# A retention and phase-mixing kernel on one core: the third pair of chunks is loaded ahead of the token weights, and the orders of the first batch are rewritten for it

## The chip, the core and the metric

The kernel runs on one core of one Trainium2 chip. Its engines work side by side, each through its own list of instructions in order: TensorE (PE in the profile, its weight loads PEld), VectorE (DVE), ScalarE (ACT), GpSimd (POOL) and SyncE (SP), which here issues the transfers. An engine waits for another through semaphores. The metric is the device time of one execution in microseconds, as the median of several runs; a profile of one execution tells what each engine did at each moment. The time before is 168.54 us (median of 3 runs, 168.21 to 168.79).

## What is computed

Two layers follow each other. The first is a retention recurrence over 768 tokens for each of 4 batches and 8 heads of 64; the second mixes its output `x` (4 x 768 x 512) over tokens, through weights that are multiplied with cosine and sine of `x @ w_theta`:

```python
for t in range(S):                                   # retention, per batch and head
    state = gamma * state + einsum('bhd,bhe->bhde', k[:, :, t], v[:, :, t])
    y[:, :, t] = scale * einsum('bhd,bhde->bhe', q[:, :, t], state)
x = y.transpose(0, 2, 1, 3).reshape(B, S, H * D)

theta = x @ w_theta                                  # phase mixing
zr, zi = x * cos(theta), x * sin(theta)
u = x + einsum('ts,bsd->btd', w_tok_r, zr) + einsum('ts,bsd->btd', w_tok_i, zi)
out = u + maximum(u @ w_ch, 0.0)
```

All inputs and the output are float32; the kernel computes in bf16 with float32 sums.

## The kernel before

The 768 tokens of a batch are 3 pairs of chunks (a chunk is 128 tokens), so there are 12 pairs, n = 0 to 11; pairs 0 to 2 are batch 0. The output has 24 tiles of 128 tokens, m = 0 to 23; the tiles of a batch need z of all its six chunks, and all token weights.

What a pair goes through, by the names of the code: `load` brings k, q and v (512 KB each). `prep` casts k to bf16 and multiplies q and v with powers of gamma (tile `kqb`); `DP` means half on DVE and half on POOL, `PP` both halves on POOL. `flip` transposes k or q on TensorE into PSUM (`kq_ps`) and copies it to `kqT`. `ret_A` makes the scores of one half of the pair, `ret_mask` masks them on DVE, `ret_Y` multiplies them with v, `ret_I` adds what comes from the state of earlier chunks, `ret_S` adds to the state and `state_out` copies it (ACT). `ret_out` copies the result to `xT`; `x_pe` transposes it back to `x_sb`; `theta` is the product with w_theta and its cosine and sine (ACT); `zmul` makes z on DVE.

What a tile goes through: `w_cast` and `w_flip` bring one row of 128 of both token weights to bf16 (POOL) and transpose it (TensorE); `moe_M(m, lo, hi)` adds the products of tile m with z of chunks lo to hi-1 (two products of 512 columns each); `moe_u` adds x; `moe_U` transposes u; `moe_O` is the product with w_ch; `moe_out` makes the output tile `ot`; `store` writes it. `keep_busy` issues products of zeros that nobody reads.

PSUM buffers are shared by tags: all transposes and the outputs of `moe_O` take turns in two buffers of the tag `tr`; retention results and theta in two of `acc`; scores have one (`at`), the state one (`st`), token products one (`y`).

```python
    def load(n, name):
        b, g = divmod(n, nG)
        t = io.tile([P, H, 2 * D], FT, name="pair", bufs=7)
        ...
    def load_wtok(r, t0):
        src = (moe_w_tok_r, moe_w_tok_i)[r]
        t = io.tile([P, S], FT, name="wtok", bufs=4)
        ...
    # p: k, q, v of a pair; w: a row of both token weights; th, ch: w_theta, w_ch
    loads("p0 th p1 w0 p2 w1 w2 p3 w3 ch p4 w4 p5 w5")
    ...
    DV, PL, AC = nc.vector, nc.gpsimd, nc.scalar
    DP, PP = (DV, PL), (PL, PL)
    ... # pair 0
    theta(0, 0)
    flip(1, "k")
    theta(0, 1)
    flip(1, "q")
    prep(1, "v", PP)
    w_cast(0)
    x_pe(0, None)
    ret_A(1, 0)
    ret_mask(1, 0)
    x_out(0, DV.tensor_copy)
    keep_busy(3)
    ret_S(1, 0)
    ... # rest of pair 1, with w_flip(0, 0) in it
    w_flip(1, 0)
    prep(2, "k", (PL,))
    zmul(0, 0)
    flip(2, "k")
    prep(2, "q", DP)
    theta(1, 0)
    zmul(0, 1)
    theta(1, 1)
    moe_M(0, 0, 1)
    flip(2, "q")
    prep(2, "v", PP)
    w_cast(1)
    w_cast(2)
    x_pe(1, AC.copy)
    moe_M(0, 1, 2)
    ret_A(2, 0)
    ret_mask(2, 0)
    ... # rest of pair 2, then token products of tiles 0 and 1, flips of pair 3

    for n in range(nG, B * nG + 1):         # n = 3 to 12
        mine, done = tiles_of[n], tiles_of[n - 1]
        ...
        if n == nG:
            nc.gpsimd.tensor_copy(wch, wdma["ch"])
        ...
        if n in pairs:
            ret_A(n, 0)
            ret_mask(n, 0)
        if n == nG:
            moe_M(0, 5, nT)
            w_flip(1, 2)
            moe_u(0)
            moe_M(1, 4, nT)
            moe_u(1)
        ...
        moe_M(first, 0, 3 if two else 2)
        ... # state, second scores, Y of pair n
        if n < U_DMA:
            moe_U(done)
        if n == nG:
            prep(n + 1, "k", (AC,))
            preps(DP)                       # q and v of pair n+1, and a w_cast
        if n == nG or n + 1 < K_DMA and not two:
            moe_M(first, 2, 4)
        if n < nG + 3:
            w_tok(n - nG + 3)               # both w_flips of a row
        if not two:
            moe_M(first, 4, nT)
            moe_u(first)
        for i, t in enumerate(done):
            if n == nG:
                flip(n + 1, "kq"[i])
            moe_O(t)
            moe_out(t)
        ...
```

Of the kernel before, what the change touches and what calls it, by code (L numbers as in the profile page):

```python
# [32 lines left out]
def kernel(  # L33
# [57 lines left out]

    def load_wtok(r, t0):
        src = (moe_w_tok_r, moe_w_tok_i)[r]
        t = io.tile([P, S], FT, name="wtok", bufs=4)
        nc.sync.dma_start(out=t, in_=src[t0 * P:(t0 + 1) * P, :])
        wdma[r, t0] = t

    def loads(order):
        for what in order.split():
            if what == "th":  # L100
                load_w512("th", moe_w_theta)
            elif what == "ch":
                load_w512("ch", moe_w_ch)
            elif what[0] == "w":
                for r in range(2):
                    load_wtok(r, int(what[1:]))
            else:
                for name in "kqv":
                    load(int(what[1:]), name)

    loads("p0 th p1 w0 p2 w1 w2 p3 w3 ch p4 w4 p5 w5")


    warm = const.tile([P, dm], BF)
# [72 lines left out]
            copy(t, ps)  # L187
        st[n, name + "T"], st[n, name + "_ps"] = t, ps

    def flip_out(n, name):  # L190
        nc.vector.tensor_copy(st[n, name + "T"], st[n, name + "_ps"])

    def flip_dma(n, name):
        t = work.tile([P, 2, NP, P], BF, name="kqT", bufs=6)
# [109 lines left out]
    def x_out(n, copy):  # L304
        b, g = divmod(n, nG)
        copy(xs[b][:, 2 * g:2 * g + 2, :],
             st[n, "x_ps"].rearrange("p a j e -> p a (j e)"))

    def theta(n, a):
        th_ps = psum.tile([P, dm], FT, name="th_ps", tag="acc", bufs=2)  # L310
        for j in range(NP):
            nc.tensor.matmul(th_ps, st[n, "xT"][:, a, j, :], wth[:, j, :], start=(j == 0),  # L312
                             stop=(j == NP - 1))
        cs = work.tile([P, 2, dm], BF, name="cs", bufs=3)
        nc.scalar.activation(cs[:, 0, :], th_ps, AF.Sin, bias=halfpi, scale=1.0)  # L315
        nc.scalar.activation(cs[:, 1, :], th_ps, AF.Sin, bias=zerob, scale=1.0)  # L316
        st[n, "cs", a] = cs
# [53 lines left out]

    def moe_out(m):
        b, t0 = divmod(m, nT)
        ot = work.tile([P, dm], FT, name="ot", bufs=8)
        nc.vector.scalar_tensor_tensor(ot, mo[m]["o"], 0.0, mo[m]["u"], ALU.max, ALU.add)  # L375
        mo[m]["ot"] = ot

# [6 lines left out]
    def w_cast(t0):  # L384
        for r in range(2):
            row = work.tile([P, S], BF, name="wrow", bufs=5)
            nc.gpsimd.tensor_copy(row, wdma[r, t0])  # L387
            wrow[r, t0] = row
# [73 lines left out]
    def keep_busy(times):  # L462
        for _ in range(times):
            nc.tensor.matmul(warm_ps, warm[:, 0:P], warm, start=True, stop=True)
# [35 lines left out]
    theta(0, 1)  # L500
    flip(1, "q")
    prep(1, "v", PP)
    w_cast(0)
    x_pe(0, None)
    ret_A(1, 0)
    ret_mask(1, 0)
    x_out(0, DV.tensor_copy)
    keep_busy(3)
    ret_S(1, 0)
    state_out(1, 0)  # L510
# [1 line left out]
    ret_mask(1, 1)  # L512
    ret_Y(1, 0)
    ret_I(1, 0)
    w_flip(0, 0)
    ret_S(1, 1)
    state_out(1, 1)
    ret_I(1, 1)
    ret_Y(1, 1)
    ret_out(1, 0, AC.copy)  # L520
    ret_out(1, 1, DV.tensor_copy)
    w_flip(1, 0)
    prep(2, "k", (PL,))
    zmul(0, 0)
    flip(2, "k")
    prep(2, "q", DP)
    theta(1, 0)
    zmul(0, 1)
    theta(1, 1)
    moe_M(0, 0, 1)  # L530
    flip(2, "q")
    prep(2, "v", PP)
    w_cast(1)
    w_cast(2)
    x_pe(1, AC.copy)
    moe_M(0, 1, 2)
    ret_A(2, 0)
    ret_mask(2, 0)
    ret_S(2, 0)
    state_out(2, 0)  # L540
    ret_A(2, 1)
    ret_mask(2, 1)
    zmul(1, 0)
    ret_Y(2, 0)
    ret_I(2, 0)
    ret_I(2, 1)
    w_flip(0, 1, False)
    w_flip(1, 1, False)
    ret_Y(2, 1)
    ret_out(2, 0, AC.copy)  # L550
    ret_out(2, 1, DV.tensor_copy)
    w_out(0, 1)
    w_out(1, 1)
    zmul(1, 1)
    prep(3, "k", (PL,))
    moe_M(0, 2, 3)
    theta(2, 0)
    flip(3, "k")
    prep(3, "q", DP)
    theta(2, 1)  # L560
    moe_M(0, 3, 4)
    x_pe(2)
    w_flip(0, 2, False)
    w_out(0, 2, AC.copy)
    moe_M(1, 0, 2)
    zmul(2, 0)
    flip(3, "q")
    prep(3, "v", PP)
    w_cast(3)
    moe_M(1, 2, 4)  # L570
    zmul(2, 1)
    moe_M(0, 4, 5)


    tiles_of = {nG - 2: [], nG - 1: [0, 1]}
# [16 lines left out]
    for n in range(nG, B * nG + 1):  # L592
# [17 lines left out]

        if n == nG:
            nc.gpsimd.tensor_copy(wch, wdma["ch"])
        if nG + 3 < n + 1 < Q_DMA:
            preps(PP)
        if late:
# [2 lines left out]
        if n in pairs:  # L618
            ret_A(n, 0)
            ret_mask(n, 0)  # L620
        if n == nG:
            moe_M(0, 5, nT)
            w_flip(1, 2)
            moe_u(0)
            moe_M(1, 4, nT)
            moe_u(1)
        if late:
            ret_Y(n - 1, 1)
            ret_S(n - 1, 1)
# [12 lines left out]
            load(n + 3, "q")  # L642

        first = mine[0]
        moe_M(first, 0, 3 if two else 2)
        if late:
            theta(n - 1, 0)
            if n - 1 < X_DMA:
# [27 lines left out]
            moe_U(done)  # L676
        if n == nG:
            prep(n + 1, "k", (AC,))
            preps(DP)
        if n == nG or n + 1 < K_DMA and not two:  # L680
            moe_M(first, 2, 4)
        early_z = late and n < nG + 3
        if early_z and n > nG + 1:
            zmul(n - 1, 0)
        if n < nG + 3:
            w_tok(n - nG + 3)
        if early_z:
            zmul(n - 1, 0 if n == nG + 1 else 1)
# [14 lines left out]
        if two and n in pairs:  # L703
            moe_u(mine[1])
        for i, t in enumerate(done):
            if n == nG:
                flip(n + 1, "kq"[i])
            moe_O(t)
            moe_out(t)
        if late and not early_z:  # L710
# [48 lines left out]
```

## Time and profile before

| What | Value |
|---|---|
| Time, median of 3 runs | 168.54 us |
| Span of the profiled execution | 166.5 us |
| TensorE busy | 155.2 us |
| VectorE busy | 102.4 us |
| ScalarE busy | 79.1 us |
| GpSimd busy | 66.6 us |
| Granted clock of TensorE | full, in all slices |
| Moved by DMA, mean | 38.45 MB, 231 GB/s |

"Busy" counts the time in which an engine had at least one instruction in work. Products on TensorE are pipelined: one of 512 columns is listed with 379 ns, while the next one starts 0.22 us later. The page cuts the span into 40 slices of 4.16 us and shows each engine's busy share in tenths. The timeline lists instructions by start and length, with the idle time ahead of them and what ended it in square brackets.

Some moments in the timeline of TensorE serve as marks. The first scores of pair 1 start at 18.34 us, those of pair 2 at 27.38, those of pair 3 at 38.25. The first iteration of the loop (n = 3) ends, and the next begins, with the `ret_I` at 48.41.

### The profile page before, as it was taken

How to read it: one execution, taken by the hardware profiler on the slowest of the kernel's cores; microseconds unless marked ns; L12 is line 12 of the kernel's file. 1: busy time of each engine (PE TensorE's matmuls, PEld its weight loads, DVE VectorE, ACT ScalarE, POOL GpSimd, SP SyncE). 2: the span in 40 equal slices, each digit the busy share in tenths (PEclk: the TensorE clock that was granted, in tenths of full speed). 3: DMA queues.
4: the chain of work that ended last, by engine and by line, in shares of the span. 5: the costliest groups of instructions: out<-in, count | busy, mean ns of one | idle time of the engine just before them, and what ended most of it. 6: DMA issues, size and time to landing. Idle time of an engine off the chain costs nothing.

```text
span 166.5 us, 4614 instructions
## 1 busy us (share of the span) xinstructions
PE 155.2 (93%) x1933; PEld 87.2 (52%) x1959; DVE 102.4 (61%) x137; ACT 79.1 (48%) x137; POOL 66.6 (40%) x82
## 2 busy tenths in 40 slices
PE   6969897899999999999999999999999999999991
PEld 2345664664755667555555554455545444444460
DVE  2257798878686699939446464584554736334442
ACT  7216568371819467687847827447083350000010
POOL 6275959786685877771442703600000000000000
PEclk9999999999999999999999999999999999999999
DMA  4999999999999999999999999998996161753343
GB/s 122 309 345 307 326 326 354 286 328 317 293 311 349 277 278 331 309 202 250 206 231 298 163 242 203 195 233 168 266 145 185 32 189 32 231 115 100 106 141 135
DMA packets 68901, 38.45 MB, mean 231 GB/s; under 512 B 26256, under 2 KB 63376, under 8 KB 68880
## 3 DMA queue, kind: packets, MB, share of 16 engines
q1 hardware_dynamic: 68736, 38.02, 90.2%
q8 instruction: 15, 0.25, 0.7%
q10 hardware_dynamic: 144, 0.13, 0.2%
q14 instruction: 6, 0.05, 0.1%
HBM read 25.69 MB, written 6.29 MB: 192 GB/s over the span
## 4 chain that ended last, share of the span: by engine, by line
PE 77%; DVE 12%; DMA 3%; issue 3%; ACT 1%; POOL 1%; DVEq 0%; SPq 0%; POOLq 0%
PE y_ps L340 33%; PE o_ps L368 12%; PE th_ps L312 11%; PE at_ps L208 4%; PE yT_ps L231 4%; DVE at L215 4%; DMA pair<-in_q_dram 3%; PE yT_ps L245 3%; PE st_ps L262 3%; PE kq_ps L183 3%; DVE z L322 2%; PE w_ps L393 2%; DVE kqT L187 2%; PE y_ps L420 2%; DVE kqb L175 1%
## 5 line engine op out<-in xcount | busy, mean ns | idle before, releaser
L340 PE MATMUL y_ps<-z,wtr 128*128 128x512 bf16 x133 | 50.5, 379 | 1.1
L340 PE MATMUL y_ps<-z,wti 128*128 128x512 bf16 x122 | 46.2, 379 | 0.4 <-issue 0.2
L347 DVE TENSOR_TENSOR u<-y_ps,x_sb 128x512 bf16<-128x512 f32 x23 | 15.9, 690 | 27.0 <-PE y_ps L340 27.0
L215 DVE TENSOR_TENSOR at<-at_ps,maskp 128x1024 bf16<-128x1024 f32 x24 | 29.3, 1221 | 4.6 <-PE at_ps L208 4.6
L175 POOL TENSOR_TENSOR kqb<-pair,qscp 128x512 bf16<-128x512 f32 x17 | 19.3, 1150 | 28.9 <-DMA pair<-in_q_dram 26.0
L175 POOL TENSOR_TENSOR kqb<-pair,vscp 128x512 bf16<-128x512 f32 x24 | 26.6, 1131 | 5.0 <-DMA pair<-in_v_dram 4.9
L285 ACT CAST xT<-yT_ps 128x512 bf16<-128x512 f32 x20 | 13.5, 739 | 30.0 <-PE yT_ps L231 29.9
L375 DVE SCALAR_TENSOR_TENSOR ot<-o_ps,u 128x512 f32<-128x512 f32 x23 | 15.9, 690 | 13.2 <-PE o_ps L368 13.2
L312 PE MATMUL th_ps<-wth,xT 128*128 128x512 bf16 x93 | 23.2, 379 | 0.5 <-ACT xT L285 0.3
L368 PE MATMUL o_ps<-wch,uT 128*128 128x512 bf16 x92 | 22.8, 379 | 0.3
L340 PEld LDWEIGHTS <-wtr 128*128 128x128 bf16 x138 | 13.5, 98 | 13.8
L276 ACT CAST stbd<-st_ps 64x256 bf16<-64x256 f32 x40 | 14.7, 368 | 12.5 <-PE st_ps L262 12.0
L340 PEld LDWEIGHTS <-wti 128*128 128x128 bf16 x138 | 13.5, 98 | 13.6 <-ACT wti L400 0.4
L315 ACT ACTIVATE cs<-th_ps,halfpi 128x512 bf16<-128x512 f32 x24 | 16.5, 689 | 7.0 <-PE th_ps L312 6.6
L322 DVE TENSOR_TENSOR z<-cs,x_sb 128x1024 bf16<-128x1024 bf16 x24 | 18.8, 808 | 0.1
L316 ACT ACTIVATE cs<-th_ps,zerob 128x512 bf16<-128x512 f32 x24 | 16.5, 687 | 0.0
L312 PEld LDWEIGHTS <-xT 128*128 128x128 bf16 x96 | 8.9, 98 | 11.0 <-ACT xT L285 1.0
L368 PEld LDWEIGHTS <-uT 128*128 128x128 bf16 x92 | 8.8, 98 | 10.5 <-issue 0.6
L208 PE MATMUL at_ps<-kqT 64*64 64x128 bf16 x384 | 10.6, 221 | 2.6 <-DVE at L215 1.8
L430 ACT COPY uT<-u_ps 128x384 bf16<-128x384 bf16 (+1 forms) x2 | 0.7, 372 | 25.5 <-PE u_ps L429 25.5
L187 DVE COPY kqT<-kq_ps 128x1024 bf16<-128x1024 bf16 x14 | 9.6, 688 | 4.2 <-PE kq_ps L183 4.1
L387 POOL CAST wrow<-wtok 128x768 bf16<-128x768 f32 x12 | 10.5, 902 | 0.3 <-DMA wtok<-in_moe_w_tok_i_dram 0.2
(61 smaller groups left out, 164.4 us busy)
## 6 DMA issues: line engine op xcount, KB each, us to landing
pair<-in_k_dram SPq DMA_DIRECT2D x12, 512.0 KB, 6.7
pair<-in_q_dram SPq DMA_DIRECT2D x12, 512.0 KB, 7.7
pair<-in_v_dram SPq DMA_DIRECT2D x12, 512.0 KB, 8.2
out_dram<-ot SPq DMA_DIRECT2D x23, 256.0 KB, 2.6
wtok<-in_moe_w_tok_r_dram SPq DMA_DIRECT2D x6, 384.0 KB, 6.4
wtok<-in_moe_w_tok_i_dram SPq DMA_DIRECT2D x6, 384.0 KB, 5.8
w<-in_moe_w_theta_dram SPq DMA_DIRECT2D x1, 1024.0 KB, 8.3
w<-in_moe_w_ch_dram SPq DMA_DIRECT2D x1, 1024.0 KB, 8.5
```

The costliest lines, as they stand in the source:

```text
L175: engines[two].tensor_mul(dst[:, two], src[:, two], _bcast_last(sc[:, 2 * g + two], D))
L208: nc.tensor.matmul(at_ps[half, par, j, :], kT[rows, two, j, half], qT[rows, :, j, half], start=(j == 0), stop=(j == NP - 1), skip_group_ch ...
L215: nc.vector.tensor_mul(at.rearrange("p a j t -> p (a j) t"), at_ps.rearrange("p a j t -> p (a j) t"), _bcast_mid(maskp[:, two].rearrange(" ...
L276: nc.scalar.copy(stbd[(c + 1) % 2][sl, :, sl], st_ps[b][sl])
L312: nc.tensor.matmul(th_ps, st[n, "xT"][:, a, j, :], wth[:, j, :], start=(j == 0), stop=(j == NP - 1))
L315: nc.scalar.activation(cs[:, 0, :], th_ps, AF.Sin, bias=halfpi, scale=1.0)
L316: nc.scalar.activation(cs[:, 1, :], th_ps, AF.Sin, bias=zerob, scale=1.0)
L322: nc.vector.tensor_mul(zs[b][:, c], st[n, "cs", a], _bcast_mid(xs[b][:, c, :], 2))
L340: nc.tensor.matmul(y_ps, wT[r][:, s0, t0 * P:(t0 + 1) * P], zs[b][:, s0, r, :], start=(s0 == 0 and r == 0), stop=(s0 == nT - 1 and r == 1))
L347: nc.vector.tensor_add(u, mo[m]["y"], xs[b][:, t0, :])
L368: nc.tensor.matmul(o_ps, mo[m]["uT"][:, j, :], wch[:, j, :], start=(j == 0), stop=(j == nD - 1))
L375: nc.vector.scalar_tensor_tensor(ot, mo[m]["o"], 0.0, mo[m]["u"], ALU.max, ALU.add)
```

## The change

The third pair of chunks (n = 2), the last of batch 0, is now loaded ahead of the first row of token weights, and w_ch ahead of the fourth row. The lists of the first batch are rewritten so that retention of pair 2 follows that of pair 1 at once, and casts, transposes and products with the token weights come behind it. For this, k of pairs 2 and 3 is copied from PSUM by ACT (`flip_out` with a choice of engine), `theta` is split into its product and its sines, with one product in the tag `y`, and there is one `keep_busy` more. In the first iteration of the loop, tiles 0 and 1 are already complete, four of the six steps of tile 2 run ahead of the state, and the fourth row of weights is transposed between the flips of k and q of pair 4, whose q is also prepared there. Buffers: five for token weights in float32 (four before), four for `cs` (three), seven for output tiles (eight). The aim is to start the dependent chain of pair 2 earlier.

```diff
-        t = io.tile([P, S], FT, name="wtok", bufs=4)
+        t = io.tile([P, S], FT, name="wtok", bufs=5)
-    loads("p0 th p1 w0 p2 w1 w2 p3 w3 ch p4 w4 p5 w5")
+    loads("p0 th p1 p2 w0 w1 w2 p3 ch w3 p4 w4 p5 w5")
...
-        cs = work.tile([P, 2, dm], BF, name="cs", bufs=3)
+        cs = work.tile([P, 2, dm], BF, name="cs", bufs=4)
-        ot = work.tile([P, dm], FT, name="ot", bufs=8)
+        ot = work.tile([P, dm], FT, name="ot", bufs=7)
... # first batch, new list from the end of pair 1 on
+    flip(2, "k", None)
+    prep(2, "q", DP)
     ret_Y(1, 1)
     ret_out(1, 0, AC.copy)
     ret_out(1, 1, DV.tensor_copy)
+    flip_out(2, "k", AC.copy)
+    keep_busy(1)
     flip(2, "q")
     prep(2, "v", PP)
+    theta(1, 0)
     ret_A(2, 0)
     ret_mask(2, 0)
+    x_pe(1)
+    theta_mm(1, 1, "y")
     ret_S(2, 0)
     state_out(2, 0)
+    sines(1, 1)
+    w_cast(0)
     ret_A(2, 1)
     ret_mask(2, 1)
     ret_Y(2, 0)
     ret_I(2, 0)
     ret_I(2, 1)
+    w_flip(0, 0)
     ret_Y(2, 1)
+    ret_out(2, 0, DV.tensor_copy)
+    ret_out(2, 1, AC.copy)
+    w_flip(1, 0)
+    w_cast(1)
+    theta(2, 0)
+    zmul(0, 0)
+    zmul(0, 1)
+    theta(2, 1)
+    zmul(1, 0)
+    x_pe(2)
+    zmul(1, 1)
+    w_cast(2)
     prep(3, "k", (PL,))
+    moe_M(0, 0, 3)
+    w_flip(0, 1)
+    w_flip(1, 1)
+    zmul(2, 0)
+    moe_M(0, 3, 4)
+    flip(3, "k", None)
+    zmul(2, 1)
+    flip_out(3, "k", AC.copy)
     prep(3, "q", DP)
+    moe_M(1, 0, 3)
+    moe_M(0, 4, nT)
     flip(3, "q")
     prep(3, "v", PP)
+    moe_u(0)
+    moe_M(1, 3, nT)
+    w_flip(0, 2)
+    w_flip(1, 2)
+    moe_u(1)
... # the loop; n == nG is its first iteration
         if n == nG:
             nc.gpsimd.tensor_copy(wch, wdma["ch"])
+            w_cast(n - nG + 3)
-        if n == nG:
-            moe_M(0, 5, nT)
-            w_flip(1, 2)
-            moe_u(0)
-            moe_M(1, 4, nT)
-            moe_u(1)
-        moe_M(first, 0, 3 if two else 2)
+        moe_M(first, 0, 3 if two else 4 if n == nG else 2)
         if n == nG:
             prep(n + 1, "k", (AC,))
-            preps(DP)
-        if n == nG or n + 1 < K_DMA and not two:
+        elif n + 1 < K_DMA and not two:
             moe_M(first, 2, 4)
-        if n < nG + 3:
+        if nG < n < nG + 3:
             w_tok(n - nG + 3)
         for i, t in enumerate(done):
-            if n == nG:
-                flip(n + 1, "kq"[i])
+            if n == nG and i == 1:
+                flip(n + 1, "k")
+                w_tok(n - nG + 3)
+                preps(DP)
+                flip(n + 1, "q")
             moe_O(t)
             moe_out(t)
```

## The prediction, made before the changed kernel was run

> **What bounds the kernel now.** I read the page first (busy shares, slices), then the windows view cut at the borders of the first batch's stages, then the timeline of each engine over the first 60 us, and last the waits of TensorE. The page:
>
> ```profile
> span 166.5 us, 4614 instructions
> PE 155.2 (93%) x1933; PEld 87.2 (52%) x1959; DVE 102.4 (61%) x137; ACT 79.1 (48%) x137; POOL 66.6 (40%) x82
> PE   6969897899999999999999999999999999999991
> PEclk9999999999999999999999999999999999999999
> DMA  4999999999999999999999999998996161753343
> ```
>
> TensorE is the bound, at full clock, and the queues are loaded nearly to the last quarter. The slices below 9 lie in the first third of the PE row (slices 1 to 9): that is the only place where this change moves instructions. By stages (columns: stretch, its length, then busy us and count for PE, PEld, DVE, ACT, POOL, then clock, DMA share, GB/s):
>
> ```profile
> 18.34:27.38 9.04, 8.57 (x155) 5.56 (x156) 8.24 (x10) 5.82 (x12) 6.57 (x7) 1.00 1.12 332
> 27.38:38.25 10.87, 9.20 (x150) 6.15 (x153) 8.82 (x12) 5.86 (x10) 9.19 (x11) 1.00 1.06 312
> 38.25:48.41 10.16, 9.80 (x131) 5.94 (x133) 7.91 (x11) 4.19 (x6) 7.19 (x7) 1.00 1.04 307
> 58.63:120.00 61.37, 60.58 (x849) 33.91 (x859) 39.63 (x51) 37.78 (x66) 25.36 (x24) 1.00 1.08 240
> ```
>
> 18.34 is the first score product of pair 1, 27.38 that of pair 2, 38.25 that of pair 3; at 48.41 the first iteration of the big loop ends. After 58.63 PE is busy 60.58 of 61.37 us: nothing to win. From 18.34 to 48.41 DVE is busy 83% (24.97 of 30.07) and the queues run at over 300 GB/s throughout. The end of this stretch, which my argument needs most, in the timeline (start, length, engine, line):
>
> ```profile
> 43.02 1.01 ACT L361 COPY uT<-u_ps 128x1024 bf16<-128x1024 bf16 x1 [0.18 <-PE u_ps L359]
> 43.93 1.05 ACT L169 CAST kqb<-pair 128x1024 bf16<-128x1024 f32 x1
> 44.09 0.69 DVE L175 TENSOR_TENSOR kqb<-pair,qscp 128x512 bf16<-128x512 f32 x1 [0.60 <-DMA pair<-in_q_dram]
> 44.20 1.48 POOL L175 TENSOR_TENSOR kqb<-pair,qscp 128x512 bf16<-128x512 f32 x1 [1.36 <-DMA pair<-in_q_dram]
> ...
> 45.30 0.61 PE L183 MATMUL kq_ps<-ident,kqb 128*128 128x128 bf16 x8
> ...
> 46.82 0.61 PE L183 MATMUL kq_ps<-ident,kqb 128*128 128x128 bf16 x8
> ...
> 47.55 1.02 PE L368 MATMUL o_ps<-wch,uT 128*128 128x512 bf16 x4
> ...
> 48.41 0.39 PE L245 MATMUL yT_ps<-kqT,stbd 128*128 128x128 bf16 x4
> ```
>
> q of pair 4 landed at about 44.1, just before it was needed; k of pair 4 one transfer (some 1.7 us, the spacing of the landings) earlier, about 42.4, but ACT took it only at 43.93, behind the copy of uT.
>
> **What the Trainium skill says.** "TensorE: Matmul & The Clock Gate", section "Back-to-back issue gap", gives N/2.4 + 2.5 ns for an isolated gap, 216 ns at N=512, and about 131 ns for a sustained stream. The trace starts successive 512-column products 0.21 to 0.22 us apart (37.08, 37.29, 37.51): the first figure holds here and the second does not, so I count 0.216. "SBUF — State Buffer", section "Who interferes with whom", says that a DVE instruction with two SBUF inputs contends with a GpSimd instruction that reads SBUF, the later one blocking. The trace agrees: the q halves on POOL take 1.04 to 1.55 us, and the z products on DVE a mean 808 ns where an undisturbed one takes 0.67. "Perfetto Trace Analysis", section "Identifying the Most-Contended Engine", warns that busy time of matmuls is no measure of headroom; so I count starts, not busy time.
>
> **How much idle there is.** The work of PE between 18.34 and 48.41, with spacings of undisturbed groups from its timeline: 36 products of L340, 16 of theta and 8 of o at 0.216 = 12.96; six k/q flips, two x flips and one u flip of 8 at 0.45 = 4.05; eight weight flips of 6 at 0.33 = 2.64; six groups of scores at 0.24, five of Y and four of inter-chunk products at 0.23, four of state at 0.30 = 4.71. Together 24.4 us in 30.07: 5.7 us of waits, 0.8 of them filled by three dummy products. That is the most that any reordering here could win; the largest shown wait is 1.07 us, PE on the mask of pair 2.
>
> **The change part by part.**
>
> *Removed and added work.* None of size: every product, flip and copy is there in both. One dummy product is added (0.22 us, in a wait), k of pairs 2 and 3 leave PSUM through ACT instead of DVE, and copies of xT, x and the weights swap engines. The ring of output tiles shrinks from 8 to 7; the stores of a tile come at least seven tiles before its buffer's next use, so I count 0.
>
> *Transfers.* Pair 2 takes the place of the first token weights. Two 384 KB transfers come out ahead of it, so its k lands near 18.7 instead of 21.8, v near 22.4 instead of 25.1. w_ch goes ahead of the fourth weight rows. Up to pair 4 the sum of bytes is the same, and the queue runs without a gap, so I let k and q of pair 4 land where they did, 42.4 and 44.1. The sixth weight tile must wait for the first cast of weights, which moves on POOL from 19.0 to about 24.5 (behind v of pair 2); with five buffers that issue waits until about 25.3, while some 3.8 us of transfers are still queued. No gap, by a margin of about 2 us.
>
> *Pair 2, up to theta(2,0).* From 18.34 the walk goes on with durations from the rows: mask 1.22, PSUM copy on ACT 1.03, xT 0.74, k/q copy on DVE 0.69. Mask(1,1) ends at 21.77 as before; Y(1,1) at 21.95; xT on ACT 22.5 to 23.2; k of pair 2 out on ACT 23.1 to 24.1; scores of pair 2 at 24.1 (before: 27.38, a gain of 3.3 us for pair 2). Then mask, scores, x copy, mask, Y: 24.6 to 25.8, 26.0, 25.7 to 26.4, 26.5 to 27.7, 27.75; xT 28.25 to 28.95; theta(2,0) at 29.0 against 32.15. But in those 10.7 us PE does only about 7.5 us of work: weights and token products were what filled these waits before, and they are now behind. PE stands idle about 3.2 us here.
>
> *The filled stretch.* From 29.0: 8 theta, 24 token products (6.91 together), one x flip, two k/q flips (1.35), four weight flips (1.32) = 9.6 us, all with inputs ready: scores of pair 3 at 38.6. Before it was 38.25, but with six token products and one weight flip (1.6 us) still to do. The changed kernel is thus ahead by 1.6 - 0.35 = 1.3 us.
>
> *The end of the first iteration.* Here the lead is given back. M(2) waits for the third weight flip's copy on ACT (38.8 to 39.6): PE idle 0.6. Its eight products to 41.2; state, scores and Y to 42.0; u flips 42.0; uT on ACT 42.6 to 43.65; k of pair 4 on ACT to 44.6 (landed 42.4, so not bound by the transfer); flip of k 44.65, a gain of 0.65. Then the new order: the copy of k leaves DVE at 46.1, the weight flips wait in turn for two PSUM buffers (45.5 and 46.15, tag of two shared with o and k/q), DVE copies weights to 46.6 and only then takes its half of q, 46.5 to 47.2. Flip of q at 47.25, against 46.82 before; last o product at 47.7; the iteration ends at 48.55, against 48.41. Some 1.4 us of idle from 43.3 on.
>
> *After that* the order on PE is the same, with 0.8 us idle in 61, so the difference stays: +0.15 us. The sum is 168.54 + 0.15 = 168.7.
>
> I put the point a little lower, at 168.4. The walk takes the longer of two durations wherever DVE and POOL meet, and it stands on k of pair 4 waiting 1.1 us for ACT: all that I overestimate before 43.6 moves the end earlier by as much, up to 1.1 us; what I underestimate moves it later in the same way. As I took the longer durations, I expect more of the first than of the second. That shift of 0.3 is judgement.
>
> **Rivals.** *The lead is kept*: if PE, being a whole pair ahead, held its 1.3 us lead, the end would be at 167.2. For it: the score wait of 1.07 us is filled, and pair 2 is 3.3 us earlier. Against it: the bytes up to q of pair 4 are not fewer, and q landing at 44.1 plus POOL's 1.5, flip 0.45, and o 0.86 cannot end much before 47.1. So 167.2 is also near the floor. *All idle removed*: 168.5 - 5.7 = 163; the same floor speaks against it. *The weights become the wait*: should the late first cast leave a gap in the queue (1 us), or the casts on POOL slip, token products and pair 4 slide: 169.5. The 2 us margin speaks against it. *Serial tail*: w_tok between the flips of k and q could cost more than I have, if POOL's v casts block DVE's half of q (0.69 becomes 1.35, seen at 61.50): 169.4.
>
> **Range and chances.** Both sides reach about 1 us: floor 167.2, bad case 169.5. Range 167.2 to 169.6, point 168.4. The 2% marks lie at 165.2 and 171.9, beyond both; faster 0.03, same 0.94, slower 0.03.
>
> **What would show it.** Scores of pair 2 near 24.1; theta(2,0) near 29.0; scores of pair 3 at 38.6; flip of q of pair 4 later than 46.8 with DVE's half of q after the weights' copy; first iteration ending 47.4 to 49.5 and the same distance from there to the end, 118.1 us. Wrong if pair 4 lands over 1 us off, if PE stays ahead through the iteration's end, or if the stretch after it takes another time.

## The result, and the profile after

| What | Before | After |
|---|---|---|
| Time, median (lowest to highest) | 168.66 us (168.21 to 169.24) | 170.74 us (170.11 to 170.79) |
| Span of the profiled execution | 166.5 us | 169.1 us |

The kernel before ran once more beside the changed one, which is why its time is not the 168.54 of the first measurement. The ratio is 1.0113, with a 95% interval of 1.0073 to 1.0152: the changed kernel is 2.1 us slower. The prediction said 168.4, in 167.2 to 169.6, and a difference of less than 2%. The difference is less than 2%; the time lies outside the range. The two profiled executions took 168.21 and 170.79 us, the shortest before and the longest after, so their marks differ by half a microsecond more than the medians.

The page of the changed kernel:

```profile
span 169.1 us, 4613 instructions
PE 155.7 (92%) x1933; PEld 86.8 (51%) x1960; DVE 104.9 (62%) x137; ACT 79.5 (47%) x137; POOL 65.5 (39%) x82
PE   7869898977979999999999999999999999999991
PEclk9999999999999999999999999999999999999999
DMA  4999997999999899999999999998958161653343
```

The amount of work is the same (155.7 us on TensorE, 155.2 before). What grew is DVE, by 2.5 us, with the same 137 instructions. The PE row gains a tenth in slices 7 and 8 (25 to 34 us) and falls from 9 to 7 in slices 9, 10 and 12 (34 to 42 and 47 to 51 us). The windows view, cut at the marks of this kernel (length of the stretch, then busy us and count of PE, PEld, DVE, ACT, POOL, then clock, DMA share, GB/s):

```profile
18.31:29.62 11.31, 10.08 (x239) 6.75 (x240) 9.28 (x12) 7.21 (x15) 8.57 (x9) 1.00 0.95 306
29.62:41.40 11.78, 9.96 (x80) 5.76 (x82) 10.72 (x12) 4.76 (x7) 8.67 (x7) 1.00 1.04 321
41.40:51.44 10.04, 8.46 (x121) 4.79 (x122) 7.10 (x10) 4.29 (x6) 7.01 (x9) 1.00 1.09 309
```

The second row decides. Between theta(2,0) at 29.62 and the scores of pair 3 at 41.40 DVE is busy 10.72 of 11.78 us and TensorE only 9.96. The kernel before had as high a share of DVE once (8.24 of 9.04, in the first of its stretches), so the share alone proves nothing; what waits for it must be looked up. The marks beside the prediction's:

| Mark | Before | Predicted | After |
|---|---|---|---|
| first scores of pair 2 | 27.38 | 24.1 | 24.48 |
| theta(2,0) | 32.15 | 29.0 | 29.62 |
| scores of pair 3 | 38.25 | 38.6 | 41.40 |
| flip of q of pair 4 | 46.82 | 47.25 | 50.12 |
| end of the first iteration | 48.41 | 48.55 | 51.44 |
| from there to the end of the span | 118.1 | 118.1 | 117.7 |

So of the 2.9 us by which the end of the first iteration misses its predicted moment, 0.6 come before theta(2,0), 2.2 in the stretch up to the scores of pair 3 (11.78 instead of 9.6), and 0.1 after it. The timeline of DVE in that stretch shows the second term (start, length, engine, line; a row with x3 or x2 is that many in a run, its length from the start of the first to the end of the last; brackets hold idle time ahead):

```profile
28.84 0.72 DVE L285 CAST xT<-yT_ps 128x512 bf16<-128x512 f32 x1
29.45 3.14 DVE L331 TENSOR_TENSOR z<-cs,x_sb 128x1024 bf16<-128x1024 bf16 x3
32.51 0.68 DVE L306 COPY x_sb<-x_ps 128x1024 bf16<-128x1024 bf16 x1
33.11 1.07 DVE L331 TENSOR_TENSOR z<-cs,x_sb 128x1024 bf16<-128x1024 bf16 x1
34.11 0.54 DVE L409 COPY wtr<-w_ps 128x768 bf16<-128x768 bf16 x1
34.58 2.80 DVE L331 TENSOR_TENSOR z<-cs,x_sb 128x1024 bf16<-128x1024 bf16 x2
37.30 1.52 DVE L175 TENSOR_TENSOR kqb<-pair,qscp 128x512 bf16<-128x512 f32 x1
```

No row carries a bracket: from 28.37, where the copy ahead of xT starts, to 38.82 DVE has no idle time. The six z take 7.01 us in these rows, where undisturbed ones take 3.8 (1.87, 0.68 and 1.28 in rows shown below), and DVE's half of q of pair 3, which took 0.68 before, takes 1.52. POOL, in the same stretch:

```profile
29.67 2.38 POOL L396 CAST wrow<-wtok 128x768 bf16<-128x768 f32 x2 [0.16 <-DMA wtok<-in_moe_w_tok_r_dram]
32.60 1.04 POOL L171 CAST kqb<-pair 128x1024 bf16<-128x1024 f32 x1 [0.56 <-DMA pair<-in_k_dram]
34.29 1.04 POOL L175 TENSOR_TENSOR kqb<-pair,qscp 128x512 bf16<-128x512 f32 x1 [0.65 <-DMA pair<-in_q_dram]
35.78 2.49 POOL L175 TENSOR_TENSOR kqb<-pair,vscp 128x512 bf16<-128x512 f32 x2 [0.45 <-DMA pair<-in_v_dram]
```

Each stretched row of DVE lies beside one of these; the two copies out of PSUM, 0.68 and 0.54 us, do not stretch. And TensorE waits for DVE:

```profile
34.24 0.38 PE L349 MATMUL y_ps<-z,wtr 128*128 128x512 bf16 x1 [0.30 <-DVE z L331]
37.43 0.38 PE L349 MATMUL y_ps<-z,wtr 128*128 128x512 bf16 x1 [0.60 <-DVE z L331]
38.88 0.62 PE L183 MATMUL kq_ps<-ident,kqb 128*128 128x128 bf16 x8 [0.86 <-DVE kqb L175]
41.40 0.42 PE L208 MATMUL at_ps<-kqT 64*64 64x128 bf16 x16
```

The last wait is the flip of q of pair 3: it waits for DVE's half of q, which stands at the end of the chain of z. That is the theory to test. Its rivals are the casts of the weights alone, the transfers, the new order at the end of the iteration, and the unfilled waits in the chain of pair 2.

### The profile page after: what moved, and what is told of

It reads as the page before. It is cut to its first block, busy times and chain, and to the rows that moved or that the text cites. A ratio compares the mean times of both kernels' runs of the same rounds, so it can differ in the third digit from the quotient of the medians.

```text
span 169.1 us, 4613 instructions
## 1 busy us (share of the span) xinstructions
PE 155.7 (92%) x1933; PEld 86.8 (51%) x1960; DVE 104.9 (62%) x137; ACT 79.5 (47%) x137; POOL 65.5 (39%) x82
## 4 chain that ended last, share of the span: by engine, by line
PE 73%; DMA 10%; DVE 7%; ACT 2%; POOL 2%; issue 2%; SPq 1%; DVEq 0%; ACTq 0%
PE y_ps L349 32%; PE o_ps L377 12%; PE th_ps L317 10%; DMA pair<-in_q_dram 5%; DMA w<-in_moe_w_theta_dram 5%; DVE z L331 4%; PE at_ps L208 3%; PE yT_ps L231 3%; PE st_ps L262 3%; PE yT_ps L245 3%; PE kq_ps L183 2%; PE y_ps L429 2%; SPq L81 1%; PE w_ps L402 1%; DVE kqb L175 1%
## 5 line engine op out<-in xcount | busy, mean ns | idle before, releaser
L175 POOL TENSOR_TENSOR kqb<-pair,qscp 128x512 bf16<-128x512 f32 x17 | 18.5, 1102 | 30.1 <-DMA pair<-in_q_dram 30.1
L175 POOL TENSOR_TENSOR kqb<-pair,vscp 128x512 bf16<-128x512 f32 x24 | 25.7, 1091 | 4.9 <-DMA pair<-in_v_dram 4.9
L317 PE MATMUL th_ps<-wth,xT 128*128 128x512 bf16 x89 | 22.2, 379 | 0.7 <-DVE xT L285 0.5
L331 DVE TENSOR_TENSOR z<-cs,x_sb 128x1024 bf16<-128x1024 bf16 x24 | 19.8, 858 | 0.0
L324 ACT ACTIVATE cs<-th_ps,halfpi 128x512 bf16<-128x512 f32 x23 | 15.8, 689 | 7.1 <-PE th_ps L317 6.6
L325 ACT ACTIVATE cs<-th_ps,zerob 128x512 bf16<-128x512 f32 x23 | 15.8, 687 | 0.0
L183 PE MATMUL kq_ps<-ident,kqb 128*128 128x128 bf16 x120 | 9.4, 220 | 2.8 <-DVE kqb L175 1.8
L396 POOL CAST wrow<-wtok 128x768 bf16<-128x768 f32 x12 | 11.1, 934 | 1.5 <-DMA wtok<-in_moe_w_tok_r_dram 0.7
```

The costliest lines, as they stand in the source:

```text
L175: engines[two].tensor_mul(dst[:, two], src[:, two], _bcast_last(sc[:, 2 * g + two], D))
L331: nc.vector.tensor_mul(zs[b][:, c], st[n, "cs", a], _bcast_mid(xs[b][:, c, :], 2))
```

## The experiments

Times are medians; ratios are to the kernel before, run beside it on the same chip, with 95% intervals; executions in a slower state, up to three of a kernel, are left out of both. In the diffs, - marks lines of the kernel that is edited. A profile is one execution; its marks are read as such.

### The casts of the weights taken out

```diff
+            if t0 in (1, 2):
+                nc.gpsimd.memset(row, 0.0)
+                nc.gpsimd.tensor_copy(row[:, 0:1], wdma[r, t0][:, 0:1])
+            else:
+                nc.gpsimd.tensor_copy(row, wdma[r, t0])
```

This leaves out the second and third row of token weights (all but one column is zero).

> The changed kernel, but the second and third row of both token weights are not cast on POOL: the bf16 tiles are set to zero there, which takes about as long and reads nothing but one column (that column keeps the wait for the landing and the release of the buffer). Output of these rows is left out. Theory A (the z products on DVE are stretched because POOL casts weights beside them): the first four z of the first batch fall from 1.09 us on average to about 0.68, all six from 7.24 us to 5.0 to 5.6; scores of pair 3 start at 39 to 40 us instead of 41.40, the first iteration ends near 49.3 instead of 51.44, and the time is about 168.7 us. Theory B (transfers: the sixth weight tile waits for its buffer and pair 4 lands 1 us later) and theory C (the order at the end of the first iteration): nothing changes, 170.7 within 0.4 us, scores of pair 3 at 41.4.

Measured: 170.07 us, 1.0097 [1.0063, 1.0132]. The scores of pair 3 start at 41.12, 0.3 us earlier than in the changed kernel, where theory A asked for 39 to 40. DVE in this kernel:

```profile
29.66 1.87 DVE L331 TENSOR_TENSOR z<-cs,x_sb 128x1024 bf16<-128x1024 bf16 x3
32.21 0.69 DVE L306 COPY x_sb<-x_ps 128x1024 bf16<-128x1024 bf16 x1 [0.67 <-PE x_ps L299]
32.81 1.03 DVE L331 TENSOR_TENSOR z<-cs,x_sb 128x1024 bf16<-128x1024 bf16 x1
34.31 2.79 DVE L331 TENSOR_TENSOR z<-cs,x_sb 128x1024 bf16<-128x1024 bf16 x2
37.02 1.52 DVE L175 TENSOR_TENSOR kqb<-pair,qscp 128x512 bf16<-128x512 f32 x1
```

The first three z fall to 1.87 us, which fits that the casts beside them had stretched them. But DVE then stands 0.67 us until TensorE has transposed x, and the second half of the stretch, beside the cast of k and the halves of q and v of pair 3, is as long as ever. The weight casts are not what binds.

### One more weight buffer

```diff
-        t = io.tile([P, S], FT, name="wtok", bufs=5)
+        t = io.tile([P, S], FT, name="wtok", bufs=6)
...
-        t = work.tile([P, 2, dm], BF, name="kqb", bufs=12)
+        t = work.tile([P, 2, dm], BF, name="kqb", bufs=11)
```

> The changed kernel with six buffers for token weights in float32 instead of five (and eleven instead of twelve for kqb, to make room), so that the sixth weight tile no longer waits for the first cast. Theory B: pair 4 lands about 1 us earlier (its q near 44.1 instead of 45.0), the first iteration ends about 1 us earlier, and the time falls to 169.7 us or less. Theory A and theory C: pair 4 lands earlier, but waits as before; the first iteration ends at 51.4 within 0.3 us, the time stays 170.7 within 0.4.

Measured: 170.19 us, 1.0133 [1.0085, 1.018] (three runs, one of 171.47). q of pair 4 landed at 43.53 instead of 45.03, and the first iteration ended at 51.01 instead of 51.44. Transfers 1.5 us earlier moved it by 0.4, and the stretch before, whose z took 6.37 us here, was 0.6 shorter: transfers do not bind here.

### The old order at the end of the first iteration

```diff
+            preps(DP)
...
-        if nG < n < nG + 3:
+        if n < nG + 3:
             w_tok(n - nG + 3)
...
-            if n == nG and i == 1:
-                flip(n + 1, "k")
-                w_tok(n - nG + 3)
-                preps(DP)
-                flip(n + 1, "q")
+            if n == nG:
+                flip(n + 1, "kq"[i])
```

> The changed kernel with the end of the first iteration in the order of before: q of pair 4 prepared ahead of the last two steps of tile 2, the fourth row of weights flipped there too, and the flips of k and q each ahead of one o product. Theory C: most of the loss comes back, the first iteration ends near 49.3, the time is about 168.8 us. Theory A: scores of pair 3 stay at 41.4; only the 1.4 us in which TensorE stood idle from the u flips on is in play, so the first iteration ends at 50.4 to 51.0 and the time is 169.8 to 170.4. Theory B: unchanged.

Measured: 169.91 us, 1.0100 [1.0061, 1.0139]. From the scores of pair 3 to the end of the iteration the profile shows 9.50 us instead of 10.04. The order costs about half a microsecond, which is not the main loss. In this execution the z happened to take 4.69 us, and the scores of pair 3 came at 40.03 without any edit there, after a stretch of 10.64 us instead of 11.78: how much DVE loses varies from execution to execution. That, and not the order alone, is why the iteration ended at 49.53, earlier than theory A's 50.4 to 51.0.

### Both halves of q of pair 3 on POOL

```diff
-    prep(3, "q", DP)
+    prep(3, "q", PP)
```

> The changed kernel with both halves of q of pair 3 multiplied on POOL instead of one on DVE. Theory A in its wider form (DVE is the chain between 28.4 and 38.8 us, and q of pair 3 stands at its end): the flip of q of pair 3 starts at 36.8 to 37.8 instead of 38.88, bound by POOL or by the second z of pair 2; scores of pair 3 at 39.5 to 40.5, the time 169.0 to 169.9 us. Theory B and theory C: 170.7 within 0.4 us.

Measured: 170.16 us, 1.0103 [1.0076, 1.013]. The stretch shrank as expected, from 11.78 to 9.87 us (29.52 to 39.39), close to the predicted 9.6. Not all of this is the edit's: the z took 4.69 us here too, and against the unedited 10.64 with the same z the edit is worth 0.8. The time missed the expected 169.0 to 169.9. The lead was partly lost in the next step, which took 10.62 us instead of 10.04:

```profile
47.04 2.49 POOL L175 TENSOR_TENSOR kqb<-pair,vscp 128x512 bf16<-128x512 f32 x2 [0.35 <-DMA pair<-in_v_dram]
47.34 1.29 DVE L175 TENSOR_TENSOR kqb<-pair,qscp 128x512 bf16<-128x512 f32 x1
48.69 0.62 PE L183 MATMUL kq_ps<-ident,kqb 128*128 128x128 bf16 x8 [1.26 <-DVE kqb L175]
```

DVE, now earlier, takes its half of q of pair 4 while POOL is in v of pair 4; that half takes 1.29 us (0.72 in the changed kernel) and TensorE waits 1.26 us for it.

### POOL's share of pair 3 taken out

```diff
+            elif n == 3:
+                nc.gpsimd.memset(t, 0.0)
+                nc.gpsimd.tensor_copy(dst[:, 0, 0, 0:1], src[:, 0, 0, 0:1])
...                                      # the same for POOL's half of q and for v
```

This leaves out k, half of q and v of pair 3 (zeros but for single columns); DVE's work is untouched.

> The changed kernel, but what POOL makes of pair 3 (the cast of k, its half of q, both halves of v) is set to zero, with one column read so that the wait for the landing stays. That part of pair 3 is left out of the output. Theory A2 (not the weight casts, but POOL's work for pair 3 stretches the last three z products of the first batch and DVE's half of q of pair 3, and the flip of q waits for that chain): the last two z and the half of q together take 2.0 to 2.9 us instead of 4.39, the flip of q of pair 3 starts at 36.6 to 37.4 instead of 38.88, scores of pair 3 at 39.2 to 39.9 instead of 41.40; as in the run with q on POOL, the end of the iteration gives part of it back, time 169.9 to 170.3 us. Rival (the order alone, DVE's list is too long whatever POOL does): flip of q of pair 3 no earlier than 38.2, time 170.7 within 0.4.

Measured: 169.81 us, 1.0082 [1.0059, 1.0105]. DVE in this kernel (lines shift by seven; L182 is the half of q):

```profile
29.66 1.97 DVE L338 TENSOR_TENSOR z<-cs,x_sb 128x1024 bf16<-128x1024 bf16 x3
32.81 0.90 DVE L338 TENSOR_TENSOR z<-cs,x_sb 128x1024 bf16<-128x1024 bf16 x1
34.31 1.28 DVE L338 TENSOR_TENSOR z<-cs,x_sb 128x1024 bf16<-128x1024 bf16 x2
35.51 0.69 DVE L182 TENSOR_TENSOR kqb<-pair,qscp 128x512 bf16<-128x512 f32 x1
```

The last three z and the half of q, which ran beside POOL's work for pair 3, fall from 5.39 us in the rows of the changed kernel to 2.87, and the stretch is 9.73 us (29.82 to 39.55). The first three z are short as well (1.97 us), but not by the edit: in this execution POOL's weight casts fell almost wholly outside them (26.21 to 29.88, then from 32.34). So the run to compare is the one without weight casts, whose first three z took 1.87: 11.30 us there, 9.73 here. That 1.6 us is what POOL's reads for pair 3 cost DVE's z and half of q, and TensorE behind them; the rest of the lost 2 us, 0.5, goes with the first three z. At the end of the iteration the profile is 1.9 us ahead of the changed kernel (49.56); the median gains only 0.6 us against the changed kernel run beside it (170.42, below). The profiled execution of this kernel, of 171.3 us, was longer than its others, with waits for transfers of 0.90 us ahead of 78.58 and 1.21 us ahead of 110.92, so nothing is read from it after 49.56.

### Both repairs, and the changed kernel again

The old order and q of pair 3 on POOL together:

> The changed kernel with q of pair 3 wholly on POOL and the end of the first iteration in the order of before. Theories A2 and C together: scores of pair 3 at 39.4, 9.5 us from there to the end of the iteration, so 48.9 against 51.44, and the time is 168.9 to 169.5 us. Rival (the two are the same wait, or transfers bind next): pair 4 lands 1 us later than before, so the iteration ends at 49.4 or later and the time is 169.7 to 170.1, no better than the order of the end alone.

Measured: 169.55 us, 1.0088 [1.0054, 1.0121]. The scores of pair 3 start at 40.33: the z took 6.68 us in this execution and the stretch 10.56. The end of the iteration came at 50.19, as the rival said. Transfers do count here: q of pair 4 landed at 45.84, DVE took its half at once and the copy of the weights behind it (46.47 to 47.02), and TensorE waited 0.28 us ahead of the flip of k at 47.08 for a PSUM buffer of the tag `tr`; from the scores of pair 3 to the end it took 9.86 us, against 9.50 with the old order alone. The changed kernel beside it, by its times alone:

> The changed kernel once more, on the chip of the runs beside it: 170.7 us within 0.4, a ratio of 1.011 to 1.014 to the kernel before; the first iteration ends at 50.9 to 51.5.

Measured: 170.42 us, 1.0126 [1.0093, 1.0159]. (In its profile, of an execution of 172.20 us, the first iteration ended at 51.98, outside the expected 50.9 to 51.5.) By the medians the two repairs bring back 0.9 of 1.9 us, by the ratios 0.6 of 2.1; the intervals overlap, so the size is uncertain.

### Two z among the masks of pair 2

On top of both repairs, the z of pair 0 move up, one ahead of the first mask of pair 2 and one between the two masks, and x of pair 1 leaves PSUM behind the second mask:

```diff
     ret_A(2, 0)
+    zmul(0, 0)
     ret_mask(2, 0)
-    x_pe(1)
+    x_pe(1, None)
     theta_mm(1, 1, "y")
+    zmul(0, 1)
...
     ret_mask(2, 1)
+    x_out(1, DV.tensor_copy)
...
-    zmul(0, 0)
-    zmul(0, 1)
```

> As the run before it, and the two z of pair 0 are made ahead of the weight casts, in gaps of DVE between the masks of pair 2, with the copy of x of pair 1 behind the second mask. Theory A2: DVE has two products less between 29.4 and 38 us, the z of pair 2 come up to 1 us earlier; but TensorE does its work there already without waits, so scores of pair 3 start at 38.6 to 39.3 and the time is 168.6 to 169.4 us. Rival (the masks of pair 2 are the tighter chain, each z ahead of one delays it): theta of pair 2 starts 0.5 to 1 us later than 29.5 and the time is 169.4 to 170.2 us.

Measured: 169.79 us, 1.0085 [1.0055, 1.0114]: nothing gained over the two repairs, as the rival said. The stretch falls from 10.56 to 9.73 us, but theta(2,0) starts at 30.92 instead of 29.77: the first z, stretched to 1.45 us, holds DVE until the mask at 25.73, and the second, of 1.16, stands ahead of the other mask. DVE's work was moved into the dependent chain, and the chain became longer by more than the stretch lost.

### The third row of weights behind pair 3; the end of the iteration once more

On top of both repairs, the third row is loaded behind pair 3 and cast behind its v:

```diff
-    loads("p0 th p1 p2 w0 w1 w2 p3 ch w3 p4 w4 p5 w5")
+    loads("p0 th p1 p2 w0 w1 p3 w2 ch w3 p4 w4 p5 w5")
...
-    w_cast(2)
     prep(3, "k", (PL,))
...
     prep(3, "v", PP)
+    w_cast(2)
```

> The kernel with q of pair 3 on POOL and the old order of the end, and beside that the third row of token weights loaded behind pair 3 and cast behind v of pair 3: no transfer waits for a cast, and no weight cast runs beside the z products. Theory B2 (with DVE's chain and the end mended, transfers bind what is left): pair 4's q lands at 44.1 to 44.8 instead of 45.8, the first iteration ends at 48.7 to 49.3 instead of 50.19, the time is 168.6 to 169.2 us, level with the kernel before. Rival D (the waits of 3.8 us in the bare chain of pair 2, between 18.3 and 29.6 us, are what is left): pair 4 lands earlier, the iteration ends at 49.8 to 50.3 all the same, the time stays at 169.5 to 170.0.

Measured: 169.39 us, 1.0065 [1.0044, 1.0087]. theta(2,0) 29.71, scores of pair 3 at 40.13, end of the iteration at 49.56. Neither forecast came true: q of pair 4 landed at 45.07, only 0.8 us earlier than in the run with both repairs, and the end came 0.6 us earlier, between the two.

The next one also transposes u of tiles 0 and 1 (`moe_U`) between the steps of tile 2, and puts one `moe_O`, the weight flips and q, v of pair 4 right behind the second scores:

> As the run before it, and a further order of the end: u of tiles 0 and 1 is transposed ahead of the state of pair 3, between the steps of tile 2, so that ScalarE has copied it before k of pair 4 lands; the first o product and the weight flips follow the second scores. If the end is a chain over ScalarE and the two shared PSUM buffers (theory C), the iteration ends 0.8 to 1.5 us earlier than in the run beside it, at 47.6 to 48.6, and the time is 167.6 to 168.6 us, at or below the kernel before. If transfers of pair 4 bind (B2), it ends no earlier than 48.3. If neither, no change against the run beside it, within 0.3.

Measured: 169.39 us, 1.0053 [1.0026, 1.008]; the marks 29.77, 40.51, 49.77: no change against the run before. The best order with pair 2 ahead is still 0.9 us behind the kernel before.

### The chain of pair 2 shortened

On top of the kernel with the third row late and the old order, the scores and masks of pair 2 are left out (zeros stand for the masked scores):

> The kernel with the third row of weights behind pair 3, q of pair 3 on POOL and the old order of the end (its time was 169.48 us), with the scores and masks of pair 2 left out: zeros take their place in its products with v, so what pair 2's tokens add to each other is missing from the output. Theory D (the waits in the bare chain of pair 2 are what is left of the loss): theta of pair 2 starts 1.2 to 2 us earlier, at 27.7 to 28.5 us instead of 29.7, the first iteration ends as much earlier, near 48.0, and the time is 167.7 to 168.4 us. Theory B2 (landings of pairs 3 and 4 bind behind it): theta of pair 2 is earlier, but the first iteration ends no earlier than 49.0 and the time stays above 169.0.

Measured: 168.85 us, 1.0011 [0.999, 1.0032]. theta(2,0) came at 29.22, only 0.5 us earlier: the expected 1.2 to 2 us did not come, so the masks are not what holds this chain up alone: without them TensorE waits 0.50 us for q of pair 2 from POOL ahead of 23.35, and 0.35 for ACT's copy of the state ahead of 27.20. The end of the iteration came 0.86 us earlier (48.70), of which some 0.5 us is the work left out. The time lies between the two forecasts. This run does not settle what the unfilled waits cost.

### The kernel before, with its filling taken out

The reverse question, on the kernel before: what did the work that filled the waits of pair 2 cost? First, the two weight flips and four token products are moved behind the chain:

```diff
-    w_flip(0, 0)
...
-    w_flip(1, 0)
...
-    moe_M(0, 0, 1)
...
-    moe_M(0, 1, 2)
...
-    moe_M(0, 2, 3)
+    w_flip(0, 0)
+    w_flip(1, 0)
+    moe_M(0, 0, 3)
```

> The kernel before, with its own transfers, but the first row's two weight flips and the first four products of tile 0 taken out of the waits of pairs 1 and 2 and made just ahead of the next two products of tile 0 (1.5 us of work on TensorE, nothing left out). Theory D (such filling is what the kernel before lives on, and the change took it away): TensorE waits instead where they stood, scores of pair 2 start at 27.4 to 27.5 all the same, and the first iteration ends 1.0 to 1.6 us later than 48.41; the time is 169.4 to 170.1 us. If the filling is worth nothing (the transfers set the pace), the time stays at 168.5 within 0.4.

Measured: 171.35 us, 1.0139 [1.0079, 1.02]. This looks like the loss of the change, but it is another one:

```profile
32.22 0.83 PE L393 MATMUL w_ps<-ident,wrow 128*128 128x128 bf16 x12 [1.48 <-ACT wti L400]
33.94 0.39 PE L340 MATMUL y_ps<-z,wti 128*128 128x512 bf16 x1 [0.89 <-ACT wti L400]
```

The moved flips take turns in the two shared PSUM buffers of the tag `tr`: TensorE waits 1.48 us for a copy out of one of them, and then a product waits 0.89 us for the transposed weights themselves. In the changed kernel TensorE's longest wait for such a copy in its first 51 us is 0.18 us. So the four products alone were moved:

> The kernel before, with only the first four products of tile 0 (0.86 us of work on TensorE) taken out of pair 2's waits and made together with the next two; the weight flips stay where they were, so the two shared PSUM buffers see the same order as before. Theory D (the waits of the dependent chain swallow such work, and outside them it costs its full length): scores of pair 2 start 0.2 to 0.4 us earlier, the first iteration ends 0.4 to 0.7 us later than 48.41, the time is 168.9 to 169.3 us. If the filling is worth nothing, the time stays at 168.5 within 0.2.

Measured: 169.19 us, 1.0029 [1.0004, 1.0054]. The sign is as the theory wants, and the size 0.5 us. But the profile shows two waits that do not come from missing filling:

```profile
27.81 0.31 PE L262 MATMUL st_ps<-kqb 64*64 64x64 bf16 x8 [0.56 <-POOL kqb L175]
33.67 0.62 PE L183 MATMUL kq_ps<-ident,kqb 128*128 128x128 bf16 x8 [0.74 <-POOL kqb L171]
```

The first is for v of pair 2, which POOL finished when it did before (27.75 against 27.63); TensorE only came to it earlier. The second is for k of pair 3, whose transfer landed at 32.34, some 1 us later than in the profile of the kernel before. Counted from the first scores of pair 1 (18.07 here, 18.34 before), the scores of pair 2 came 0.4 us earlier, and theta(2,0), ahead of which the same products are now done, at the same distance (13.83 and 13.81 us). In this profile, then, the moved products cost nothing up to there; the loss comes behind it, with k of pair 3 and with q of pair 4, which landed at 45.27 instead of 44.07. Whether that holds for the median is not shown.

Last, an attempt on the kernel before: the second z behind the copy of q on DVE, and two products into the wait for the mask.

```diff
-    zmul(0, 1)
     theta(1, 1)
     moe_M(0, 0, 1)
     flip(2, "q")
+    zmul(0, 1)
...
-    moe_M(0, 1, 2)
     ret_A(2, 0)
...
+    moe_M(0, 1, 2)
```

> The kernel before, with the second z of pair 0 made on DVE behind the copy of q of pair 2 instead of ahead of it, where POOL's multiplication of v stretches it to 1.54 us, and with the two products that need it moved from ahead of pair 2's scores into the wait for the first mask of pair 2. From theories A2 and D together: scores of pair 2 start at 26.6 to 27.0 us instead of 27.38, the wait of 1.07 us shrinks to 0.6, the first iteration ends 0.4 to 1.0 us earlier, the time is 167.6 to 168.1 us, better than both kernels. If q of pair 4, landing near 44.1, binds the end of the iteration (theory B2), no gain over 0.3.

Measured: 168.66 us, 1.0020 [0.9995, 1.0046]. No gain: scores of pair 2 came at 27.06, the wait for the mask shrank to 0.76, but then TensorE waited 0.64 us for the next z, which took 1.19 beside POOL's weight casts. No version tried is faster than the kernel before.

## Why the prediction was wrong

*The bound and the place: right.* TensorE at full clock, the loss confined to the first 51 us, and 117.7 us after it against 118.1 predicted. The smaller ring of output tiles cost nothing that shows.

*Pair 2, up to theta(2,0): mechanism right, 0.6 us short.* Scores at 24.48 (24.1), theta(2,0) at 29.62 (29.0). The gain of about 3 us for pair 2 is there. The walk let the scores follow k of pair 2, whose copy on ACT ended at 24.15, as predicted. But they waited for q: it landed at 21.61, POOL's half of it took until 23.23, and its copy on DVE ended at 24.42.

*The filled stretch: this step failed.* The prediction wrote "= 9.6 us, all with inputs ready: scores of pair 3 at 38.6". The inputs were not ready. The sum of TensorE's work was right to 0.1 us: with POOL's share of pair 3 taken out, TensorE goes through the stretch without a wait in 9.73 us. But the walk followed only TensorE here, and took for granted that DVE, with POOL beside it, would keep pace. The change gathers the six z of the first batch between 29.45 and 37.4 us, in the very time in which POOL casts weights and prepares pair 3, and hangs DVE's half of q at the end of that run. These are the runs with all six z in the stretch (z is the sum of their rows in the timeline of DVE):

| Kernel | half of q of pair 3 on DVE | z, us | stretch, us |
|---|---|---|---|
| changed | 1.52 us | 7.01 | 11.78 |
| six weight buffers | 1.53 us | 6.37 | 11.15 |
| weights taken out | 1.52 us | 5.69 | 11.30 |
| old order at the end | 1.53 us | 4.69 | 10.64 |
| pair 3 taken out | 0.69 us | 4.15 | 9.73 |
| q on POOL | none | 4.69 | 9.87 |
| both repairs, third row late | none | 6.67 | 10.42 |
| both repairs | none | 6.68 | 10.56 |
| third row late, u early | none | 6.99 | 10.74 |
| third row late, chain shortened | none | 6.31 | 10.05 |

At equal z the half of q costs 0.8 to 1.0 us (10.64 against 9.87; 11.78 against 10.74); the z, from 4.69 to 6.99, cost another 0.9. The z do not all count alike: in the run without weight casts the first three were short, and the stretch is 11.30 all the same. The changed kernel's own trace gives the same sizes. Against the 9.73 us without waits, TensorE's starts fall back at three places only: by 0.47 and 0.56 us at products that need a new z (34.24 and 37.43), and by 1.02 at the flip of q (38.88). Together 2.05, and 0.13 by which the sum was short: the 2.2 us missed. The prediction had the mechanism in hand: it named the z at 0.67 and at a mean of 808 ns, quoted the contention, and even took "the longer of two durations wherever DVE and POOL meet" elsewhere, but not in this stretch.

*The end of the first iteration: right in length, by luck in part.* 10.04 us against 9.95. The old order takes 9.50 in one run, so the rival of a serial tail is worth half a microsecond. Its detail was off: DVE's half of q of pair 4 was expected to take 0.7 us at 46.5 and took 0.72 at 49.34, when POOL's v of pair 4 (46.70 to 48.74) was over; in the run with q of pair 3 on POOL it met that v and took 1.29.

*Transfers: right where it mattered for the changed kernel.* The issue of the sixth weight tile did stall, from 22.3 to 26.6 us, until the first cast had freed a buffer, later than the predicted 25.3. Its data still landed 1.07 us behind the fifth's, at the normal spacing: no gap from it. q of pair 4 landed at 45.03 instead of 44.1. Yet with the loads of the kernel before, it landed at 44.07, 43.40, 45.27 and 44.01 in four executions, so a difference of 1 us is within what one profile can differ from the next. And one buffer more did not bring the time back. In the run with both repairs q of pair 4 did hold TensorE up, by some 0.4 us.

*Rivals.* That the weights become the wait was given 169.5 and fell with the experiments without casts and with one more buffer. That the lead is kept was wrong: the 1.3 us of lead had turned into a deficit at the scores of pair 3.

*The range.* It reached 1.2 us above the point, built from single rival effects. None of them moved the chain of the filled stretch from TensorE to DVE, and two at once were not added.

*What stays open.* The best repaired kernel keeps 0.9 us, 1.0053 [1.0026, 1.008]. Its marks put it in places that the prediction knew: 0.8 us more than predicted before theta(2,0), and 1.1 more in the stretch, whose z are still 6.99 us, less 0.7 won at the end. In its trace the z account for 1.0 of the 1.1 us: against the stretch without waits TensorE's starts fall back by 0.40, 0.35 and 0.26 us, each time at a product that starts 0.05 us after the z that it needs has ended (33.22, 34.67 and 37.57). No run took these waits away with the repairs in place. What the unfilled chain of pair 2 costs by itself isn't settled: moving filling out of the kernel before was confused by PSUM waits or by late transfers, and leaving work out of the chain gave less than expected. Nor do the marks carry over in full: q on POOL gained 1.4 us at the end of the iteration in its profile (50.01 against 51.44), but its median stands 1.70 us above the kernel before, against 2.08 and 1.94 for the changed kernel: a gain of 0.2 to 0.4. Taking out POOL's share of pair 3 gained 0.6. The z took 4.69 us in one profile and 7.01 in another of kernels that are alike up to there, so the 2.2 us are the loss of one profiled execution; how much of the 2.1 us between the medians is this chain, beyond these gains, is not shown.

## What to carry to other kernels

When a reordering gathers work that used to be spread, walk every engine through the new stretch, not only the one that is the bound: a stretch that is full on TensorE needs its suppliers to keep pace, at their disturbed durations. Ask which instruction stands last in the supplier's list, because what it feeds (here one half of q) waits for the whole run ahead of it. The sign in a profile is a timeline of the supplier without a single bracket, with the bound engine's brackets naming it. Take more than one profile before trusting the size: the same list of instructions lost 0.9 us in one execution and 2.05 in another.

## What the runs showed of the hardware

The Trainium skill, "SBUF — State Buffer", section "Who interferes with whom", says that a DVE instruction with two SBUF inputs contends with GpSimd instructions that read SBUF, and not with those that only write. Both halves show here, with sizes the prediction lacked. A z of 128x1024 takes 0.67 to 0.68 us alone and up to 1.57 beside POOL's casts and multiplications; a half of q on DVE takes 0.69 alone and 1.52 beside v on POOL. With memsets on POOL in place of weight casts, the first three z take 0.67, 0.68 and 0.68. Copies from PSUM on DVE (0.54 to 0.72 us) did not stretch in the timelines shown.

The page also says that issue order decides who blocks, and that too can be seen. Where the z came out short beside POOL, POOL came out long:

```profile
32.38 1.58 POOL L171 CAST kqb<-pair 128x1024 bf16<-128x1024 f32 x1 [0.59 <-DMA pair<-in_k_dram]
33.88 2.13 DVE L331 TENSOR_TENSOR z<-cs,x_sb 128x1024 bf16<-128x1024 bf16 x2
34.03 1.43 POOL L175 TENSOR_TENSOR kqb<-pair,qscp 128x512 bf16<-128x512 f32 x1
```

This is the kernel with the old order at the end, whose z took 4.69 us. The z at 33.88 (0.68 us, the first of the two) started ahead of POOL's half of q, and POOL took 1.43. In the changed kernel POOL's half of q started first, at 34.29, and took 1.04, and the z that started behind it at 34.58 took 1.30. Nothing in the program differs between the two up to there; which engine starts first, and so which one pays, differed from one execution to the other.
